# Two score tiles summed in turn at a change of token group, and one weight read issued earlier

## The chip, the cores and the metric

The kernel runs on one core of a Trainium2 chip. The metric is the time of one execution on the device in microseconds (us), the median of several runs. A profile is taken of one execution; its span goes from the first to the last instruction. Engines are called PE (TensorE, matmuls), DVE (VectorE), ACT (ScalarE), POOL (GpSimd, here mostly indirect gathers) and SP (SyncE, here the queue that issues almost all other DMAs).

## The reference

A layer norm, then the sum of the input, an attention with one key/value head and 32 query heads, and a product-key mixture of experts with 32 heads and two experts of 4096 per head and token. S = 2048 tokens, D = 512.

```python
x = A_x
xn = _layernorm(x, axis=-1)
return x + _A_ref(xn, A_wq, A_wk, A_wv, A_wo) + _B_ref(xn, B_w_q, B_k1, B_k2, B_u, B_v)

# _A_ref: softmax(q k^T * Dh**-0.5) v, 32 query heads of 16, one k and one v, then wo
# _B_ref
s1 = jnp.einsum("nhd,ed->nhe", q1, k1)          # 64 keys each
s2 = jnp.einsum("nhd,ed->nhe", q2, k2)
i1 = jnp.argsort(-s1, axis=-1)[..., :K]         # K = 2
i2 = jnp.argsort(-s2, axis=-1)[..., :K]
...
g = _softmax(top_s, axis=-1)
act = _gelu(jnp.einsum("nd,nhkd->nhk", xf, u[top_e]))
out = jnp.einsum("nhk,nhk,nhkd->nd", g, act, v[top_e])
```

## The kernel before, in words

**Tokens, groups, chunks.** The 2048 tokens are 16 tiles of 128, in four groups (`ph` 0 to 3) of four tiles (`GT` = `TPH` = 4). The expert scores of a group are made in eight chunks (`c`) of four heads: the query projection and the keys are folded beforehand into one weight of 512 columns per chunk (`wp_make`), which is kept as a high and a low part, written to DRAM (`d_w`) and read again by `wp_read` for the later groups. A chunk's weight is four tiles `wk`, one per quarter of D (`KC` = 4), out of eight buffers.

**One score tile** (`item`, lines 513 to 550) is one token tile against one chunk: four quarters `k` of three matmuls each (`TERMS`: high x high, high x low, low x high; line 532) into one PSUM tile `psc` of 128x512. It needs `XT[g][k]`, the transposed normed tokens of the group (tile `xt`, four buffers, one per quarter), and `WC[n_][k]`, the chunk's weights. Then DVE takes eight `max` (line 545) and eight `max_index` (line 547), and behind the group's fourth tile `batch` combines the results into expert numbers and gates. `psc` comes out of a PSUM pool of three buffers (tag "x") which the other helpers share.

**The order of the chunks** is `SEQ`: group 0 chunks 0 to 7, group 1 chunks 0 and 1, group 2 chunks 0 to 7, group 1 chunks 2 to 7, group 3 chunks 0 to 7. Groups 0 and 1 (`NSP` = 2) use their experts by gathers of u and v rows (POOL, line 883) with DVE dot products (895) and adds (930). Groups 2 and 3 are computed densely over all experts by `dense`, behind their eighth chunk: one-hot matmuls for the gates, then 32 blocks of `pact` (line 799) and, two blocks behind each other, `pout` in `sums` (line 783).

**The hand-written order.** From line 1147 on, PE, ACT, DVE, POOL and SP run in the order in which the program emits. The loop runs over 256 attention steps. A step emits scores `sc` (318), ACT's exps `pt` (321), `pv` (332), `mid` (DVE's expert work), scores again, and at its end `fill`, which takes work from the generator `score_thread` until a budget (`aim`, at most `MOST` = 4.0 per step) is spent. The generator yields the cost of each piece, 3 x `UNIT` for a quarter. A `yield None` ends the fill of this step whatever is left in the budget.

**A turn.** While the last tile of a group's run of chunks is summed, each quarter `k` that is done frees `xt` `k`, and `load_phase2_xt` (line 994) issues the load of the next group's `xt` on SP behind it. Lines 1012 and 1013 then end the step by a `yield None` (the rest) before the next group's first tile. This holds for three turns: group 0 to 1, 1 to 2, 1 to 3. It does not hold where `dense` comes next.

**Behind the dense blocks of group 2** the chunk `after` (group 1, chunk 2) follows. Its first two weight tiles are read at the last block (line 807), its other two at the very end of `dense` (lines 862 to 864):

```python
        yield from sums()
        if after is not None:
            wp_read(after, range(2, KC))
```

SP issues DMAs strictly in the order of emission, and its queue also carries the attention's small loads and stores: `qa` (305 to 310), sums and outputs of a unit (350, 356), `rc` (365), `dinv` (371), `rsb` (376), `wo` (392).

Of the kernel before, what the change touches and what calls it, by code (L numbers as in the profile page):

```python
# [23 lines left out]
P = 128  # L24
# [4 lines left out]
E = 64  # L29
NT = S // P  # L30
GT = 4
NGRP = NT // GT
KC = D // P
NC = 8
TPH = GT
NPH = NGRP
NSP = 2
# [13 lines left out]
UNIT = 0.235  # L51
# [3 lines left out]
def tile_kernel(ctx, tc, x, wq, wkv, wo, wqT, kT, uv, ub, vb, out):  # L55
    nc = tc.nc
# [7 lines left out]
    start = start_stack.enter_context(tc.tile_pool(name="start", bufs=1))  # L64
# [55 lines left out]
    xtile = lambda name: ps.tile([P, 512], F32, name=name, tag="x", bufs=3)  # L120
# [3 lines left out]
    XT, XN, ACC, XP = {}, {}, {}, [None]  # L124
# [60 lines left out]
    TERMS = ((0, 0), (0, 1), (1, 0))  # L185
# [278 lines left out]
    WC = {}  # L464
# [37 lines left out]
    def wp_read(n, ks=range(KC)):  # L502
        for k in ks:
            wk = wk_tile()
            nc.sync.dma_start(raw(wk[:]), d_w[SEQ[n][1]][:, k])
            WC.setdefault(n, []).append(wk)

    SEQ = ([(0, c) for c in range(NC)] + [(1, c) for c in range(2)] + [(2, c) for c in range(NC)]
           + [(1, c) for c in range(2, NC)] + [(3, c) for c in range(NC)])
    M8, I8 = {}, {}  # L510
    BT = 4

    def item(n_, ti, make=()):
        ph, c = SEQ[n_]
        nph, nc_ = SEQ[n_ + 1] if n_ + 1 < len(SEQ) else (None, None)
        t = TPH * ph + ti
        g, j = divmod(t, GT)
        b, jb = divmod(ti, BT)
        if jb == 0:
            m8 = small.tile([P, BT, 8, 8], F32, name="m8", bufs=1)  # L520
            i8 = small.tile([P, BT, 8, 8], U32, name="i8", bufs=1)
            M8[ph, c, b], I8[ph, c, b] = m8, i8
        m8, i8 = M8[ph, c, b], I8[ph, c, b]
        p = xtile("psc")

        last = ti == TPH - 1
        more = nc_ is not None and not (ph >= NSP and c == NC - 1)
        read = more and n_ + 1 >= NC
        n = 0
        for k in range(KC):  # L530
            for a, bb in TERMS:
                nc.tensor.matmul(p, XT[g][k][:, a, j * P:(j + 1) * P], WC[n_][k][:, bb, :],  # L532
                                 start=n == 0, stop=n == 11)
                n += 1
            if read and ti == 0 and k < 2:
                wp_read(n_ + 1, range(2 * k, 2 * k + 2))
            if last and more and nph != ph:
                load_phase2_xt(nph, k)
            if k < KC - 1:
                yield 3 * UNIT  # L540
            if k == 1:

                yield from islice(make, 1)
        for s in range(8):
            nc.vector.max(m8[:, jb, s, :], p[:, s * E:(s + 1) * E])  # L545
        for s in range(8):
            nc.vector.max_index(i8[:, jb, s, :], m8[:, jb, s, :], p[:, s * E:(s + 1) * E])  # L547
        if jb == BT - 1:
            batch(ph, c, b)
        yield 3 * UNIT  # L550

    IDX, G = {}, {}
# [9 lines left out]
                DT.append(da[:, i, :].rearrange("p (t r s) -> p t r s", t=GT, r=2))  # L562

    def batch(ph, c, b):
        m8, i8 = M8.pop((ph, c, b)), I8.pop((ph, c, b))
        sh = [P, BT, 4]
        T = lambda name, dt=F32, s=sh, bufs=1: small.tile(s, dt, name=name, bufs=bufs)
        mv = m8.rearrange("p t (h s) k -> p t h s k", s=2)
        a1, a2, b1, b2 = mv[:, :, :, 0, 0], mv[:, :, :, 0, 1], mv[:, :, :, 1, 0], mv[:, :, :, 1, 1]
        s1, c1, c2, cond = T("s1"), T("c1"), T("c2"), T("cond")  # L570
        V = nc.vector
        V.tensor_add(s1, a1, b1)
        V.tensor_add(c1, a1, b2)
        V.tensor_add(c2, a2, b1)
        V.tensor_tensor(out=cond, in0=c1, in1=c2, op=OP.is_ge)
        mx = T("mx")
        V.tensor_max(mx, c1, c2)
        V.tensor_sub(mx, mx, s1)
        ex = T("ex")

        def exp_later(gates):

            def go():
                nc.scalar.activation(ex, mx, AF.Exp)
                behind(gates)

            LATER.append(go)

        fi = T("fi", F32, [P, BT, 8, 2])
        V.tensor_copy(fi, i8[:, :, :, 0:2])  # L590
        fv = fi.rearrange("p t (h s) k -> p t h s k", s=2)
        i1a, i1b, i2a, i2b = fv[:, :, :, 0, 0], fv[:, :, :, 0, 1], fv[:, :, :, 1, 0], fv[:, :, :, 1, 1]
        e1, e2 = T("e1"), T("e2")
        stt = V.scalar_tensor_tensor
        den = T("den")
        if ph < NSP:
            idx = T("idx", I32, [P, BT, 4, 2], NIDX)
            stt(idx[:, :, :, 0], i1a, float(E), i2a, op0=OP.mult, op1=OP.add)
            stt(e1, i1a, float(E), i2b, op0=OP.mult, op1=OP.add)
            stt(e2, i1b, float(E), i2a, op0=OP.mult, op1=OP.add)  # L600
            V.tensor_sub(e1, e1, e2)
            V.tensor_mul(e1, e1, cond)
            V.tensor_add(idx[:, :, :, 1], e1, e2)
            gg = T("gg", F32, [P, BT, 4, 2], NIDX)

            def gates():
                V.tensor_scalar(den, ex, 2.0, 2.0, op0=OP.mult, op1=OP.add)
                V.reciprocal(gg[:, :, :, 0], den)
                V.tensor_mul(gg[:, :, :, 1], ex, gg[:, :, :, 0])
                G[ph, c] = gg  # L610

            exp_later(gates)
            for jb in range(BT):
                IDX[ph, c, b * BT + jb] = idx[:, jb].rearrange("p h k -> p (h k)")
            return
        w = slice(8 * c, 8 * c + 8)
        if c == 0:
            DT.clear()
            dense_tiles()
        df1, df2, dgt = DT[:3]  # L620
        ii = T("ii", F32, [P, 2, BT, 8])
        for n, (p0, p1, q0) in enumerate(((i1b, i1a, i1a), (i2a, i2b, i2a))):
            o = ii[:, n].rearrange("p t (h k) -> p t h k", k=2)
            V.tensor_copy(o[:, :, :, 0], q0)
            V.tensor_sub(e1, p1, p0)
            V.tensor_mul(e1, e1, cond)
            V.tensor_add(o[:, :, :, 1], e1, p0)
        hi = T("hi", F32, [P, BT, 8])
        V.tensor_scalar(hi, ii[:, 1], 32.0, None, op0=OP.is_ge)
        for r in range(2):  # L630
            stt(df1[:, :, r, w], hi, 64.0, ii[:, 0], op0=OP.mult, op1=OP.add)
            stt(df2[:, :, r, w], hi, -32.0, ii[:, 1], op0=OP.mult, op1=OP.add)

        def gates():
            V.tensor_scalar(den, ex, 2.0, 2.0, op0=OP.mult, op1=OP.add)
            gg = T("gd", F32, [P, BT, 8])
            gv = gg.rearrange("p t (h k) -> p t h k", k=2)
            V.reciprocal(gv[:, :, :, 0], den)
            V.tensor_mul(gv[:, :, :, 1], ex, gv[:, :, :, 0])
            gh = T("gh", F16, [P, BT, 8])  # L640
            V.tensor_scalar(gh, gg, GS, None, op0=OP.mult)
            V.tensor_copy(dgt[:, :, 0, w], gh)
            stt(dgt[:, :, 1, w], gg, GS, gh, op0=OP.mult, op1=OP.subtract)

        exp_later(gates)


    def dense(DG, after):
# [60 lines left out]
        for n, src in enumerate((df1, df2, dgt)):  # L709
            if n == 2:  # L710
                yield None
            p = xtile("ptd")
# [60 lines left out]
        def sums():  # L773

            used[0] += 2
            if formed[0] < used[0]:
                flush()
            for j in range(GT):
                p = xtile("pout")
                n = 0  # L780
                for wd, vs in ready:
                    for a, c in TERMS:
                        nc.tensor.matmul(p, wd[:, a, j * P:(j + 1) * P], vs[:, c, :], start=n == 0, stop=n == 5)  # L783
                        n += 1
                acc = ACC[GT * DG + j]
                nc.vector.tensor_add(acc, acc, p)  # L786
                yield 6 * UNIT
# [3 lines left out]
        for b in range(NB):  # L791
# [4 lines left out]
            n = 0  # L796
# [58 lines left out]
            if b % 2:  # L855
# [3 lines left out]
                else:  # L859
                    yield None  # L860
                ready, held = held, []
        yield from sums()
        if after is not None:
            wp_read(after, range(2, KC))
        OUTS.extend(range(GT * DG, GT * DG + GT))


# [133 lines left out]
    def score_thread():  # L1001
        for n, (ph, c) in enumerate(SEQ):
            if n < 2:
                yield from wp_make(c)
            make = wp_make(n + 1) if 0 < n < NC - 1 else iter(())
            for ti in range(TPH):
                yield from item(n, ti, make)
                yield from islice(make, 1)
            yield from make
            WC.pop(n)  # L1010
            if n + 1 < len(SEQ) and SEQ[n + 1][0] != ph and not (ph >= NSP and c == NC - 1):
                yield None
            if ph >= NSP and c == NC - 1:
                yield from dense(ph, n + 1 if n + 1 < len(SEQ) else None)
                dense_on[0] = 0
# [246 lines left out]
```

## Time and profile before

| | |
|---|---|
| median of three runs | 1997.14 us (1992.95, 1997.14, 2001.03) |
| the profiled execution | 2001.03 us, its span 1999.3 us, mean granted clock 0.967 |
| DVE busy | 1682.7 us (84% of the span) |
| ACT busy | 1292.0 us (65%) |
| POOL busy | 570.8 us (29%) |
| score matmuls `psc` | 1536, 388.2 us in all |
| `pv` and `sc` matmuls of the attention | 4096 and 2048, 524.1 and 389.1 us |

A timeline row reads: start in us, length in us, engine, line, operation, output<-inputs, shapes, count, and in brackets the idle time of the engine before it with what ended that. A row of SP (SPq) is the issue of DMAs, not their transfer. A windows row reads: stretch, its length, then busy us of PE, PEld (weight loads, which overlap PE), DVE, ACT and POOL with counts, the granted TensorE clock, the DMA engines' busy share, and GB/s. In the chain of work that ended last, PE has 63% of the span and DVE 20%. The row `psc` of the groups' list names 5.3 us of idle time in front of it, 3.2 of them ended by the load of `xt`.

### The profile page before, as it was taken

To read this page: it belongs to the slowest core of one execution; us is meant where nothing else is said; L and a number is where in the kernel's file an instruction comes from. 1 tells how busy PE (TensorE), PEld (TensorE's weight loads), DVE (VectorE), ACT (ScalarE), POOL (GpSimd) and SP (SyncE) were. 2 spreads that over 40 slices of the span, in tenths; PEclk is the share of its full clock that TensorE was granted. 3 is DMA by queue.
4 is the path that set the end of the run, shared out by engine and by line. 5 is a ranking of instruction groups with operands and counts; after the bars stand their busy time and mean duration, and the time that the engine had idled before them with its cause. 6 is when DMAs were issued, how large, how long until landed. Compare 5 with 4: busy or idle time off the path is not lost.

```text
span 1999.3 us, 34729 instructions
## 1 busy us (share of the span) xinstructions
PE 1882.9 (94%) x10990; PEld 997.5 (50%) x10990; DVE 1682.7 (84%) x6713; ACT 1292.0 (65%) x1804; POOL 570.8 (29%) x542
## 2 busy tenths in 40 slices
PE   6869999999998998999999999999899789999997
PEld 4534444555554444555555455555445345555552
DVE  7537888999998786999999779999999668999993
ACT  3236666655556785787877565555568567788873
POOL 2202232222222232333444222222223333333320
PEclk9989999999997998999999999999979899999999
DMA  7847878977664878888889877777568877888762
GB/s 272 301 185 235 276 272 272 331 275 248 218 212 140 229 221 271 264 269 269 284 297 328 286 253 261 268 238 225 176 169 234 276 245 263 268 277 257 263 211 63
DMA packets 239882, 494.79 MB, mean 247 GB/s; under 512 B 93380, under 2 KB 93380, under 8 KB 239692
## 3 DMA queue, kind: packets, MB, share of 16 engines
q0 software_dynamic: 73728, 268.47, 40.5%
q1 hardware_dynamic: 163960, 222.44, 34.0%
q10 hardware_dynamic: 2004, 1.61, 0.3%
q8 instruction: 88, 1.44, 0.3%
q14 instruction: 102, 0.84, 0.1%
HBM read 429.51 MB, written 57.64 MB: 244 GB/s over the span
## 4 chain that ended last, share of the span: by engine, by line
PE 63%; DVE 20%; DMA 5%; issue 2%; ACT 2%; SPq 1%; DVEq 0%; ACTq 0%
PE pv L332 18%; PE sc L318 12%; PE psc L532 10%; PE pout L783 8%; PE pact L799 8%; DVE i L547 5%; DVE xa L930 4%; DVE m L545 3%; DVE g L895 3%; PE pg L752 3%; PE pw L487 2%; PE pwo L427 1%; DMA dg<-gst 1%; ACT pt L321 1%; DMA fin<-dpart 1%
## 5 line engine op out<-in xcount | busy, mean ns | idle before, releaser
L321 ACT ACTIVATE pt<-sc 128x1024 f32<-128x1024 f32 x1024 | 993.0, 1025 | 471.1 <-PE sc L318 424.6
L883 POOL DMA_INDIRECT g<-in_uv_dram,idx x512 | 554.0, 1082 | 1358.4 <-DVE xa L930 697.4
L332 PE MATMUL pv<-pt,vaug 128*32 128x512 f32 x4096 | 524.1, 631 | 0.0
L318 PE MATMUL sc<-qa,kaug 64*128 64x512 f32 x2048 | 389.1, 454 | 14.4 <-ACT pt L321 13.5
L532 PE MATMUL psc<-wk,xt 128*128 128x512 f32 x1536 | 388.2, 400 | 5.3 <-DMA xt<-dxt 3.2
L930 DVE SCALAR_TENSOR_TENSOR xa<-g,w,xa 128x512 f32<-128x512 f32 x512 | 370.6, 745 | 0.0
L895 DVE CUSTOM_DVE_ANT_0 g<-g,xa 128x512 f32<-128x512 f32 x512 | 336.1, 681 | 3.0 <-DMA g<-in_uv_dram,idx 3.0
L532 PEld LDWEIGHTS psc<-wk,xt 128*128 128x128 f32 x1536 | 277.8, 188 | 108.7 <-issue 38.5
L318 PEld LDWEIGHTS sc<-qa,kaug 64*128 64x128 f32 x2048 | 157.6, 187 | 338.2 <-ACT pt L321 203.5
L332 PEld LDWEIGHTS pv<-pt,vaug 128*32 128x32 f32 x4096 | 110.7, 113 | 263.4 <-issue 261.7
L799 PE MATMUL pact<-xt,wk 128*128 128x512 f32 x768 | 198.7, 404 | 14.6 <-DVE fin L433 6.3
L547 DVE FIND_INDEX8 i<-m,psc 128x8 uint32<-128x64 f32 x1024 | 206.4, 221 | 0.0
L783 PE MATMUL pout<-wk,wd 128*128 128x512 f32 x768 | 195.7, 402 | 8.7 <-DVE wd L835 4.7
L799 PEld LDWEIGHTS pact<-xt,wk 128*128 128x128 f32 x768 | 141.1, 190 | 65.4 <-issue 17.7
L783 PEld LDWEIGHTS pout<-wk,wd 128*128 128x128 f32 x768 | 140.6, 188 | 56.7 <-DVE wd L835 6.0
L545 DVE MAX8 m<-psc 128x8 f32<-128x64 f32 x1024 | 146.0, 214 | 22.2 <-PE psc L532 19.8
L786 DVE TENSOR_TENSOR da<-da,pout 128x512 f32<-128x512 f32 x128 | 82.7, 679 | 8.2 <-PE pout L783 7.9
L918 DVE SCALAR_TENSOR_TENSOR w<-gth,ga 128x4 f32<-128x4 f32 x128 | 20.2, 158 | 79.9 <-ACT gth L911 79.4
L688 DVE TENSOR_TENSOR wk<-rw,wk 128x512 fp32r<-128x512 f32 x128 | 84.8, 682 | 0.1
L725 DVE TENSOR_TENSOR oh<-oh 128x2048 f16<-128x2048 f16 x64 | 78.0, 1219 | 7.1 <-PE pg L752 7.1
L752 PE MATMUL pg<-oh 128*128 128x32 f16 x1024 | 73.4, 246 | 8.1 <-DVE oh L728 8.1
L687 ACT CAST wk<-rw 128x512 fp32r<-128x512 f32 x128 | 73.6, 628 | 9.0 <-DMA rw<-in_ub_dram 6.7
(150 smaller groups left out, 1341.8 us busy)
## 6 DMA issues: line engine op xcount, KB each, us to landing
wk<-dw SPq DMA_DIRECT2D x96, 512.0 KB
wqt<-in_wqT_dram SPq DMA_DIRECT2D x32, 512.0 KB
dw<-wk SPq DMA_DIRECT2D x32, 512.0 KB
rw<-in_ub_dram SPq DMA_DIRECT2D x64, 256.0 KB
rw<-in_vb_dram SPq DMA_DIRECT2D x64, 256.0 KB
dg<-gst SPq DMA_DIRECT2D x32, 512.0 KB
gy<-dg SPq DMA_DIRECT2D x64, 256.0 KB
qa<-dqh SPq DMA_DIRECT2D x128, 64.0 KB
```

The lines of the kernel that those rows point to most:

```text
L318: nc.tensor.matmul(p[:, b, :], kaug[o:o + 64, kc * P:(kc + 1) * P], QA[u][o:o + 64, i, :], start=True, stop=True)
L321: nc.scalar.activation(pt, p, AF.Exp, scale=SCALE)
L332: nc.tensor.matmul(PV[u][32 * j:32 * j + 32, :], vaug[:, kc, :], pt[:, b, :], start=kc == 0, stop=kc == 15)
L532: nc.tensor.matmul(p, XT[g][k][:, a, j * P:(j + 1) * P], WC[n_][k][:, bb, :], start=n == 0, stop=n == 11)
L545: nc.vector.max(m8[:, jb, s, :], p[:, s * E:(s + 1) * E])
L547: nc.vector.max_index(i8[:, jb, s, :], m8[:, jb, s, :], p[:, s * E:(s + 1) * E])
L752: nc.tensor.matmul(p[:, i * NB:(i + 1) * NB], oa[:, :, i], ob[:, :, i], start=True, stop=True)
L783: nc.tensor.matmul(p, wd[:, a, j * P:(j + 1) * P], vs[:, c, :], start=n == 0, stop=n == 5)
L799: nc.tensor.matmul(p, us[:, a, k * P:(k + 1) * P], XT[DG][k][:, c, :], start=n == 0, stop=n == 11)
L883: nc.gpsimd.indirect_dma_start(out=gt, out_offset=None, in_=uv, in_offset=bass.IndirectOffsetOnAxis(ap=IDX[ph, c, ti][:, s:s + 1], axis=0))
L895: nc.vector.tensor_tensor_reduce(u, u, XN[TPH * ph + ti], scale=1.0, scalar=0.0, op0=OP.mult, op1=OP.add, accum_out=a[:, i:i + 1])
L930: nc.vector.scalar_tensor_tensor(acc, v, w[:, i:i + 1], acc, op0=OP.mult, op1=OP.add)
```

## The change

`item` takes a tuple of tiles instead of one. At a turn, the last two tiles of the last chunk go through it together: for each quarter `k`, three matmuls for the third tile, three for the fourth, then the load of the next group's `xt` `k`; the two PSUM tiles are held side by side, and the maxima of both follow behind the last quarter. The `yield None` behind a turn is removed. All other tiles go one by one, as before. In `dense`, the read of the second pair of weight tiles stands in front of the last `sums` instead of behind it.

```diff
-    def item(n_, ti, make=()):
+    def item(n_, tis, make=()):
...
-        p = xtile("psc")
-        last = ti == TPH - 1
+        ps_ = [xtile("psc") for _ in tis]
+        last = tis[-1] == TPH - 1
...
         for k in range(KC):
-            for a, bb in TERMS:
-                nc.tensor.matmul(p, XT[g][k][:, a, j * P:(j + 1) * P], WC[n_][k][:, bb, :],
-                                 start=n == 0, stop=n == 11)
-                n += 1
-            if read and ti == 0 and k < 2:
+            for p, ti in zip(ps_, tis):
+                for n, (a, bb) in enumerate(TERMS):
+                    nc.tensor.matmul(p, XT[g][k][:, a, ti * P:(ti + 1) * P], WC[n_][k][:, bb, :],
+                                     start=k == 0 and n == 0, stop=k == KC - 1 and n == len(TERMS) - 1)
+                if ti != tis[-1]:
+                    yield 3 * UNIT
+            if read and tis[0] == 0 and k < 2:
                 wp_read(n_ + 1, range(2 * k, 2 * k + 2))
             if last and more and nph != ph:
                 load_phase2_xt(nph, k)
...
-        for s in range(8):
-            nc.vector.max(m8[:, jb, s, :], p[:, s * E:(s + 1) * E])
-        for s in range(8):
-            nc.vector.max_index(i8[:, jb, s, :], m8[:, jb, s, :], p[:, s * E:(s + 1) * E])
-        if jb == BT - 1:
-            batch(ph, c, b)
+        for p, ti in zip(ps_, tis):
+            for s in range(8):
+                nc.vector.max(m8[:, ti, s, :], p[:, s * E:(s + 1) * E])
+            for s in range(8):
+                nc.vector.max_index(i8[:, ti, s, :], m8[:, ti, s, :], p[:, s * E:(s + 1) * E])
+        if last:
+            batch(ph, c, 0)
...
@@ dense
-        yield from sums()
         if after is not None:
             wp_read(after, range(2, KC))
+        yield from sums()
...
@@ score_thread
-            for ti in range(TPH):
-                yield from item(n, ti, make)
+            turn = n + 1 < len(SEQ) and SEQ[n + 1][0] != ph and not (ph >= NSP and c == NC - 1)
+            for tis in ((0,), (1,), (2, 3)) if turn else ((0,), (1,), (2,), (3,)):
+                yield from item(n, tis, make)
                 yield from islice(make, 1)
             yield from make
             WC.pop(n)
-            if n + 1 < len(SEQ) and SEQ[n + 1][0] != ph and not (ph >= NSP and c == NC - 1):
-                yield None
```

More of the change, by code (lines that the diff above doesn't have):

```diff
@@ L511, in tile_kernel @@
     BT = 4
-    def item(n_, ti, make=()):
+    def item(n_, tis, make=()):
         ph, c = SEQ[n_]
         nph, nc_ = SEQ[n_ + 1] if n_ + 1 < len(SEQ) else (None, None)
[L516 to L519, printed above, removed]
+        g = ph
+        if tis[0] == 0:
             m8 = small.tile([P, BT, 8, 8], F32, name="m8", bufs=1)
             i8 = small.tile([P, BT, 8, 8], U32, name="i8", bufs=1)
-            M8[ph, c, b], I8[ph, c, b] = m8, i8
-        m8, i8 = M8[ph, c, b], I8[ph, c, b]
-        p = xtile("psc")
-        last = ti == TPH - 1
+            M8[ph, c], I8[ph, c] = m8, i8
+        m8, i8 = M8[ph, c], I8[ph, c]
+        ps_ = [xtile("psc") for _ in tis]
+        last = tis[-1] == TPH - 1
         more = nc_ is not None and not (ph >= NSP and c == NC - 1)
         read = more and n_ + 1 >= NC
-        n = 0
         for k in range(KC):
-            for a, bb in TERMS:
-                nc.tensor.matmul(p, XT[g][k][:, a, j * P:(j + 1) * P], WC[n_][k][:, bb, :],
-                                 start=n == 0, stop=n == 11)
-                n += 1
-            if read and ti == 0 and k < 2:
+            for p, ti in zip(ps_, tis):
[5 more added lines that the diff above has]
+            if read and tis[0] == 0 and k < 2:
                 wp_read(n_ + 1, range(2 * k, 2 * k + 2))
@@ L564, in batch @@
     def batch(ph, c, b):
-        m8, i8 = M8.pop((ph, c, b)), I8.pop((ph, c, b))
+        m8, i8 = M8.pop((ph, c)), I8.pop((ph, c))
         sh = [P, BT, 4]
```

## The prediction

> **What bounds the kernel now.** I read the busy totals first, then the PE timeline round the three places that the change touches, then SP's and DVE's rows there, then the windows behind them.
>
> ```profile
> PE 1882.9 (94%) x10990; PEld 997.5 (50%) x10990; DVE 1682.7 (84%) x6713; ACT 1292.0 (65%) x1804; POOL 570.8 (29%) x542
> 450.00:600.00 150.00, 150.00 (x860) 83.08 (x860) 146.70 (x977) 85.94 (x104) 36.60 (x37) 1.00 0.70 226
> 1300.00:1440.00 140.00, 140.00 (x802) 77.71 (x804) 136.79 (x900) 80.35 (x98) 34.32 (x34) 1.00 0.67 220
> ```
>
> PE is the bound: 94% of the span, and in the two long scoring stretches it is never idle (150.00 of 150, 140.00 of 140; columns are stretch, PE, PEld, DVE, ACT, POOL, clock, DMA share, GB/s). DVE is a close second there (146.70 and 136.79). So time can only come from places where PE sits idle. The groups' turns are such places. There are three: from group 0 to 1 (turn 1), from 1 to 2 (turn 2, two chunks later), from 1 to 3 (turn 3).
>
> ```profile
> 379.67 1.92 PE L332 MATMUL pv<-pt,vaug 128*32 128x512 f32 x16
> 381.53 0.73 PE L318 MATMUL sc<-qa,kaug 64*128 64x512 f32 x4
> 383.23 0.49 PE L318 MATMUL sc<-qa,kaug 64*128 64x512 f32 x2 [0.97 <-ACT pt L321]
> 384.14 0.49 PE L318 MATMUL sc<-qa,kaug 64*128 64x512 f32 x2 [0.42 <-ACT pt L321]
> ...
> 424.52 1.66 PE L532 MATMUL psc<-wk,xt 128*128 128x512 f32 x6
> ...
> 429.39 2.35 PE L532 MATMUL psc<-wk,xt 128*128 128x512 f32 x9
> 433.51 2.34 PE L532 MATMUL psc<-wk,xt 128*128 128x512 f32 x9 [1.77 <-DMA xt<-dxt]
> ```
> ```profile
> 1266.82 0.96 PE L532 MATMUL psc<-wk,xt 128*128 128x512 f32 x3
> 1267.84 0.51 PE L318 MATMUL sc<-qa,kaug 64*128 64x512 f32 x2
> 1268.75 0.50 PE L318 MATMUL sc<-qa,kaug 64*128 64x512 f32 x2 [0.41 <-ACT pt L321]
> ...
> 1275.53 2.32 PE L532 MATMUL psc<-wk,xt 128*128 128x512 f32 x9 [1.48 <-DMA xt<-dxt]
> ```
>
> Turn 1's rest leaves an attention step with no score matmuls, and PE waits for ACT: 0.97 + 0.42. Turn 2's rest cuts a step to 6 score matmuls and costs nothing itself; but the fourth quarter of the next group comes 1.77 late. Turn 3 loses 0.41 behind its rest and 1.48 for the same load. In all 1.39 + 1.77 + 1.89 = 5.05 us, 0.25% of the span: all that the first edit can take away directly.
>
> **The change part by part.** *What moves.* In the built programs ACT's and POOL's orders are unchanged. PE's differ in attention steps 33 to 44 (turns 1 and 2) and 158 to 163 (turn 3) of 256 only, DVE's and SP's in the same places, and SP's also at the second edit. The counts are the same: nothing is added, so the price is in waits alone. Steps of 0, 18, 18, 18 score matmuls become 15, 15, 15, 18; a quarter (3 matmuls) takes 3.63/15 x 3 = 0.725 us (a fill of 15 runs from 375.38 to the next row at 379.01).
>
> *When the loads go out and land.*
>
> ```profile
> 377.07 2.39 SPq L998 DMA_DIRECT2D xt<-dxt  x4
> ...
> 425.50 1.02 SPq L998 DMA_DIRECT2D xt<-dxt  x2
> ...
> 1262.38 5.75 SPq L998 DMA_DIRECT2D xt<-dxt  x4
> ```
>
> From the SP queue's packet records (a load ends in sixteen 4-byte packets) I read landings. Alone, 512 KB land 3.0 us after issue (377.07 to 380.04, 420.76 to 423.83). With gathers on the DMA engines too, loads land 2.56 us apart (1267.32, 1269.88, 1272.44, 1275.00), and the fourth of a turn 8.5, 7.2 and 7.2 us after its issue (387.61, 433.37, 1275.00). After the change quarter k of the old xt is free after quarter k of both last tiles, so the first three loads go out 0.7 to 5.5 us sooner. The fourth still leaves only after the very last quarter, and without a rest its user is 3 quarters behind.
>
> *Turn 1:* the last quarter ends with step 32 at 379.0, as before. The new group starts behind attention at 382.2, needs its fourth load at 382.2 + 3 x 0.725 = 384.4. Loads two to four leave at about 376.2, 377.6, 379.1; of the three, about 1.5 are through when gathers start at 380.0 (one of four was, starting 0.9 later), the rest take 1.5 x 2.56: landed 383.8. No wait, 0.6 to spare. Gain 1.39; ACT's exps of that step are hidden under 3.63 us of score matmuls.
>
> *Turn 2:* step 39 starts at 421.34 - 1.39 + 3 x 0.24 = 420.7 (three matmuls more are behind it than before). Its fill, from 423.9, holds the last quarter and four of the new group; the fourth load leaves at 424.6 + 0.15 and is wanted at 426.8. The rsb load, ahead of it on SP, goes out about 1.5 us sooner than at 421.85 and is through; gathers brought data from 429.0. So it lands after 3.0 us, 427.75: a wait of 1.0. Bounds: 0.8 (no issue delay) and 5.1 (7.2 as before). I take 1.0, since the queue is empty then.
>
> *Turn 3:* the last quarter is the first of step 158's fill and ends at 1267.55; the fourth load leaves by 1267.75 and is wanted at 1269.7. Gathers are in flight, so I take the shared rate: start of data 0.95 after issue, 2.56 for the transfer, some 0.2 behind: 1271.5, a wait of 1.8. Bounds: 1.0 (3.0 alone) and 5.2 (7.2). This one eats turn 3's 1.89.
>
> *PE in sum:* -5.05 + 0 + 1.0 + 1.8 = -2.25 us.
>
> *DVE.* Two tiles are now reduced behind each other, after the second. One tile's max and index take 2.66 us (tile to tile, 377.86 to 380.52). In turn 1 DVE was ready at 377.86 and now waits for 378.4: 0.55 lost. DVE sat idle for PE and ACT at 396.26 (0.70), 420.08 (1.37), 424.00 (0.58), 434.51 (0.73): 3.4, of which the three PE waits, 2.8, go as scores come sooner. 2.8 - 0.55 = 2.25 covers PE's gain of turns 1 and 2 with nothing over. PSUM: two of three score buffers are held for 8 quarters; the next group's first tile takes the third, its second tile starts a step later (6.8 us in turns 1 and 2; 0.7 + the wait in turn 3), when DVE, which in turn 3 is free of the earlier tile's 2.66 us, has just let go. Cost 0, bounds 0 to 2.66 once, in turn 3.
>
> *Second edit.* It acts once, behind group 2's dense blocks. Two 512 KB loads leave SP at about 1094 instead of 1104 to 1106, in front of rsb and wo. They were in time before: PE went from the last output sums to the scores at 1110.38 with no wait. Gain 0. Behind them on SP the rsb load (1100.49) waits for dinv's landing anyway; if their 1 MB delays it by 2 x 1.5 us, its user on DVE (L381 at 1111.18) still has some 5 us. Cost 0; bounds -0.3 and +2.
>
> *Sum.* The profiled execution took 2001.03 (span 1999.3 and 1.7 round it), 3.9 over the median of 1997.14. -2.25 makes it 1998.8, and the median 1994.9.
>
> *A clock price.* Waits can cost more than themselves:
>
> ```profile
> 601.41 0.68 PE L318 MATMUL sc<-qa,kaug 64*128 64x512 f32 x2 [0.94 <-ACT pt L321]
> 602.33 0.55 PE L318 MATMUL sc<-qa,kaug 64*128 64x512 f32 x2 [0.24 <-ACT pt L321]
> 602.80 3.51 PE L332 MATMUL pv<-pt,vaug 128*32 128x512 f32 x16
> ```
>
> Behind 1.2 us of waiting the 16 pv matmuls take 3.51 instead of 1.92 (granted clock 0.58 from 602 to 606). The 1.39 at 383 had no such follower, nor 1.48 at 1275 (1.00 in both). So each new wait costs 0 to 1.6 more; I take 0, by the nearest rows in size and place. The Trainium skill (TensorE: Matmul & The Clock Gate, "What's actually happening") says that the clock halves only after at least one idle window of about 3.4 us. By that rule neither new wait could cost it and the sum stays; the row at 602.80 contradicts it. With 1.6 for each of the two new waits the sum would be +0.95.
>
> **The rivals.**
> - *The fourth load stays as late as it was (slower).* If it again lands 7.2 us after issue in turns 2 and 3, the waits are 5.1 + 5.2 = 10.3, less 5.05: +5.3; both exceed 3.4 us and would halve the clock once each, 1.6 each: +8.5. 2002.4 to 2005.6. It decides from a mean landing of 4.7 us after issue. For it: 8.5, 7.2 and 7.2 measured. Against: in those, two or three loads issued within 2.4 us stood ahead of it; now they left 1.5 us apart, the first a step earlier.
> - *DVE becomes the bound (no change).* It ran 146.70 of 150, and before the dense blocks PE waits for its last batch:
>
> ```profile
> 1451.04 1.97 PE L714 MATMUL ptd<-ident,da 128*128 128x128 f32 x8 [8.69 <-DVE da L631]
> ```
>   If DVE ends its scores no sooner, PE's gain becomes a longer wait there and at 607.69 (0.72 now): 1997.1. For it: a balance of 2.25 gained by DVE against 2.16 gained by PE in turns 1 and 2. Against: PE's own idle of 0.00 behind each turn.
> - *All of it (faster).* The fourth loads arrive in time: -5.05, 1992.1. Against: 3.0 us is the fastest landing seen, 2.2 are there.
> - *Nothing of it shows:* that is the second edit, within every case above.
>
> **How the numbers follow.** The sum 0.42; late load 0.18; DVE 0.18; all of it 0.17; something unseen 0.05. The three runs before lie 8 us apart, so a median of three may be off by some 3. Predicted 1994.9. 80%: down from 1992.1 to 1988, up to 2005, which leaves half of the clock's price and the unseen out. 0.5% (10 us) is about what a measurement of this kernel tells from no change: faster would be below 1987.2, slower above 2007.1. No case lies there by its own price. Faster gets a quarter of "all of it" (rests that halve the clock in executions other than the profiled one) and most of the unseen, 0.08; slower a third of the late load (the clock halved for longer than one stretch) and the rest, 0.08; the same 0.84.
>
> **What would show it.** The ACT waits behind sc in steps 33 and 158 gone; one wait for xt in front of the fourth quarter in turn 2 (about 1.0) and in turn 3 (about 1.8), none in turn 1; the waits at the first ptd of both dense parts unchanged within 0.5; no wait for wk in front of group 1's third chunk, as now. A xt wait over 4 us, half clock behind a turn, or ptd waits grown by 2 would make the sum wrong.

## The result and the profile after

The changed kernel is slower. Its median is 2008.61 us over 20 runs (1998.77 to 2020.54), that of the kernel before 1997.45 over as many (1992.61 to 2009.10): a ratio of 1.005, 95% interval 1.0032 to 1.0068, or about +10 us (the two medians lie 11.2 apart). The prediction was 1994.9, range 1988 to 2005.

Line numbers of the changed kernel stand one lower or one higher than before (532 is 531, 918 is 919), those of the experiments up to ten higher. The page of the changed kernel: the chain of work that ended last, and the group of score matmuls (busy us, mean ns, idle time in front of them and what ended most of it).

```profile
PE 56%; DVE 25%; DMA 6%; issue 3%; ACT 2%; SPq 1%; ACTq 0%; DVEq 0%
...
L531 PE MATMUL psc<-wk,xt 128*128 128x512 f32 x1536 | 393.7, 403 | 11.6 <-DMA xt<-dxt 7.1
```

PE's share of the chain falls from 63 to 56%, DVE's rises from 20 to 25; the idle time in front of the score matmuls is 11.6 us instead of 5.3, of which the load of `xt` ended 7.1 instead of 3.2. PE's timeline at the three turns, in order:

```profile
387.31 2.50 PE L531 MATMUL psc<-wk,xt 128*128 128x512 f32 x9
391.51 2.35 PE L531 MATMUL psc<-wk,xt 128*128 128x512 f32 x6 [1.70 <-DMA xt<-dxt]
393.79 1.22 PE L318 MATMUL sc<-qa,kaug 64*128 64x512 f32 x4
394.94 2.24 PE L332 MATMUL pv<-pt,vaug 128*32 128x512 f32 x16
...
436.89 0.96 PE L531 MATMUL psc<-wk,xt 128*128 128x512 f32 x3 [1.38 <-DMA xt<-dxt]
...
1280.73 0.93 PE L531 MATMUL psc<-wk,xt 128*128 128x512 f32 x3 [0.69 <-DMA xt<-dxt]
1285.05 2.93 PE L531 MATMUL psc<-wk,xt 128*128 128x512 f32 x6 [3.38 <-DMA xt<-dxt]
1287.91 1.22 PE L318 MATMUL sc<-qa,kaug 64*128 64x512 f32 x4
```

The ACT waits behind `sc` are gone, but PE now waits 1.70 + 1.38 + 0.69 + 3.38 = 7.15 us for `xt`. Behind two of these waits, 1.70 and 3.38, the granted clock halves (called half clock below): four `sc` matmuls take 1.22 instead of 0.73. DVE at the same places (turn 2, then turn 3):

```profile
431.98 0.16 DVE L919 SCALAR_TENSOR_TENSOR w<-gth,ga 128x4 f32<-128x4 f32 x1 [4.33 <-ACT gth L912]
...
1278.71 1.15 DVE L546 MAX8 m<-psc 128x8 f32<-128x64 f32 x8 [1.28 <-PE psc L531]
...
1286.73 1.15 DVE L546 MAX8 m<-psc 128x8 f32<-128x64 f32 x8 [3.36 <-PE psc L531]
```

DVE waits 4.33 us for ACT's tanh in turn 2 and 1.28 + 3.36 us for score tiles in turn 3.

Most of the program isn't touched, and there one execution differs from the next by 10 us and more (1560.6 us outside the stretches below in the changed kernel, 1537.4 in the run e1 of the next section, which has the same program there). So I compare the stretches that hold the turns: attention steps 31 to 64 (turns 1 and 2) and 154 to 184 (turn 3), cut where a step's first exp begins on ACT. The last lines of the windows views over these stretches (sum of the lengths, then busy us of each engine in them), first of before, then of after:

```profile
sum 448.60, PE 434.81 PEld 240.66 DVE 430.71 ACT 253.46 POOL 109.10; mean PE 86.96 PEld 48.13 DVE 86.14 ACT 50.69 POOL 21.82
```
```profile
sum 458.20, PE 439.59 PEld 241.43 DVE 430.62 ACT 254.06 POOL 109.22; mean PE 87.92 PEld 48.29 DVE 86.12 ACT 50.81 POOL 21.84
```

They grew by 9.6 us, about the measured loss of 10. On PE's side the account closes: 4.8 us are busy time (439.59 - 434.81 for the same 2487 matmuls), 4.8 idle (18.6 instead of 13.8). Of the busy part, 4.1 lie in steps 31 to 64 and 154 to 165, where the clock was halved for 10.2 us and before not at all. The other 0.6 lies in steps 165 to 184, where after has no more half clock than before (7.2 us, 8.1 before); it isn't explained. The idle part is +3.90 of `xt` waits (7.15 - 3.25), -1.80 of ACT waits, and +2.77 of waits for DVE: 1.11 in front of `psc` at 562.84, 0.44 + 0.96 at 1364.18 and 1413.79, and 0.26 more at the first `ptd` behind turn 3 (8.95 after 8.69). DVE did the same work to within 0.1 us and sat idle 9.7 longer.

### The profile page after: what moved, and what is told of

Read it like the earlier page. It is cut to its first block, busy times and chain, and to the rows that moved or that the text cites. A ratio compares the mean times of both kernels' runs of the same rounds, so it can differ in the third digit from the quotient of the medians.

```text
span 2018.8 us, 34729 instructions
## 1 busy us (share of the span) xinstructions
PE 1887.7 (94%) x10990; PEld 1003.3 (50%) x10990; DVE 1682.7 (83%) x6713; ACT 1292.1 (64%) x1804; POOL 573.6 (28%) x542
## 4 chain that ended last, share of the span: by engine, by line
PE 56%; DVE 25%; DMA 6%; issue 3%; ACT 2%; SPq 1%; ACTq 0%; DVEq 0%
PE pv L332 15%; PE sc L318 11%; PE psc L531 9%; PE pout L784 8%; PE pact L800 7%; DVE i L548 5%; DVE xa L931 5%; DVE g L896 4%; DVE m L546 3%; DMA dg<-gst 2%; DVE oh L726 2%; PE pg L753 2%; PE pw L487 2%; PE pwo L427 1%; ACT pt L321 1%
## 5 line engine op out<-in xcount | busy, mean ns | idle before, releaser
L332 PE MATMUL pv<-pt,vaug 128*32 128x512 f32 x4096 | 512.9, 619 | 0.0
L531 PE MATMUL psc<-wk,xt 128*128 128x512 f32 x1536 | 393.7, 403 | 11.6 <-DMA xt<-dxt 7.1
L548 DVE MATCH_VALUE_LOAD i<-m,psc 128x8 f32 x1024 | 81.4, 79 | 0.0
```

What stands on the lines that cost most here:

```text
L332: nc.tensor.matmul(PV[u][32 * j:32 * j + 32, :], vaug[:, kc, :], pt[:, b, :], start=kc == 0, stop=kc == 15)
L531: nc.tensor.matmul(p, XT[g][k][:, a, ti * P:(ti + 1) * P], WC[n_][k][:, bb, :], start=k == 0 and n == 0, stop=k == KC - 1 and n == len(TER ...
L548: nc.vector.max_index(i8[:, ti, s, :], m8[:, ti, s, :], p[:, s * E:(s + 1) * E])
```

## The experiments

In this table "xt waits" is PE's waiting for the token loads in the three turns, "half" the time at half clock in the steps 31 to 64 and 154 to 165, the two lengths are those of the stretches above, from one profile each, and the ratio is to the kernel before, run beside it. The third line runs before's own program in the turns and differs from before by 0.5 and 0.2 us there: that much is noise. All times in us.

| kernel | xt waits | half | steps 31–64 | steps 154–184 | ratio, 95% interval |
|---|---|---|---|---|---|
| before | 3.25 | 0 | 231.8 | 216.8 | |
| after | 7.15 | 10.2 | 234.9 | 223.3 | 1.005 [1.0032, 1.0068] |
| e1 second edit only | 3.38 | 0 | 232.3 | 217.0 | 0.9983 [0.9962, 1.0003] |
| e2 rest put back | 0 | 0 | 232.3 | 215.5 | 0.9974 [0.9949, 0.9998] |
| e3 rest taken away only | 11.10 | 13.6 | 240.2 | 222.3 | 1.0071 [1.0047, 1.0096] |
| e4 fourth load left out | 1.05 | 0 | 231.8 | 217.5 | 0.9979 [0.9949, 1.0009] |
| e6 maxima in one bunch | 2.88 | 0 | 233.3 | 216.8 | 0.9990 [0.9964, 1.0016] |
| e5 gathers held | 7.85 | 6.8 | 235.8 | 222.2 | 1.0030 [1.0009, 1.0051] |
| e8 gathers held sooner | 7.29 | 10.2 | 234.8 | 222.9 | 1.0037 [1.0012, 1.0063] |
| e10 before, gathers held | 1.24 | 3.4 | 231.4 | 216.9 | 0.9984 [0.9957, 1.0011] |
| e11 no burst of gathers | 2.49 | 0 | 231.4 | 218.0 | 0.9984 [0.9965, 1.0003] |
| e7 buffers lent, all turns | 1.08 | 0 | 228.6 | 217.6 | 1.0032 [1.0004, 1.0059] |
| e9 buffers lent, turns 1, 2 | 1.28 | 0 | 228.5 | 216.7 | 1.0005 [0.9983, 1.0026] |
| e12 lent for a shorter time | 0 | 0 | 229.3 | 215.7 | 0.9977 [0.9955, 0.9999] |

**The parts of the change.** e1 is before with the second edit alone; e2 is after with the rest back; e3 is before without its rest, tiles one by one.

```diff
# e1, on before
-        yield from sums()
         if after is not None:
             wp_read(after, range(2, KC))
+        yield from sums()
# e2, on after
             WC.pop(n)
+            if turn:
+                yield None
# e3, on before
-            if n + 1 < len(SEQ) and SEQ[n + 1][0] != ph and not (ph >= NSP and c == NC - 1):
-                yield None
```

> The second edit alone: the two weight loads in front of the last sums, the turns as before. If the loss sits in the turns (late fourth load, or DVE starved by the bunched tiles), this run equals the kernel before: ratio 1.000 within 0.003, no wait of the scores for wk behind group 2's dense blocks, as before. If the second edit costs (its 1 MB in front of rsb and wo on SP), it is slower by some 5 us (ratio 1.0025), with a wait of DVE's L381 for rsb or of PE's L427 for wo that before does not have.

> The changed kernel with the rest put back behind each turn: two tiles in turn, then the step ends. Theory late load: the rest gives the fourth load an attention part (3.2 us) more, the waits for xt (1.70, 1.38, 0.69 + 3.38 in the changed kernel) fall under 1 in sum, and the time comes to that of before or 2 us under it (ratio 0.998 to 1.000). Theory bunching: DVE gets no finished tile for 8 quarters and then two at once, so its idle time round the turns stays some 5 us above that of before, and so does the time (ratio 1.0025) although no load is waited for.

> The kernel before without the rest: the last tiles one by one, the next group straight behind. Theory late load: all four loads go out within the last tile's four quarters and are wanted 3 quarters later, so the waits for xt are longer than in the changed kernel, 4 us or more per turn, DVE idles with PE, and the run is slower than the changed kernel (ratio to before 1.006 or more). Theory bunching: DVE gets its tiles evenly, the run is as fast as before or faster (0.997 to 1.000).

The second edit costs nothing that shows. With the rest, the in-turn order does what it was written for: no wait for `xt` is left in any turn. Without the rest PE waits in all three, in either order. So the removed rest carries the loss, and the in-turn order softens it (11.10 to 7.15 us of waits). e2 also shows the limit of the gain: PE's 1.77 of turn 2 are gone, yet steps 31 to 64 are no shorter.

**What the time follows.** e4 leaves out the fourth load of each turn, so that the next group's fourth quarter of scores is made of the old group's tokens. e6 is before, with the third tile's maxima at a turn kept back and taken together with the fourth's: the bunching alone, no other part of the change.

```diff
# e4, on after
             if last and more and nph != ph:
-                load_phase2_xt(nph, k)
+                if k < KC - 1:
+                    load_phase2_xt(nph, k)
+                else:
+                    XT[nph].append(XT[g][k])
# e6, on before (maxima() holds the two loops of max and max_index)
+        if ti == TPH - 2 and more and nph != ph:
+            KEPT.append(maxima)
+        else:
+            while KEPT:
+                KEPT.pop(0)()
+            maxima()
```

> The changed kernel, but at a turn the fourth quarter of xt is not loaded again: the next group reads the old group's fourth quarter (that quarter of its scores is computed from other tokens, and three loads of 512 KB are left out). Theory late load: no wait for the fourth quarter, at most 0.7 for the third, no half clock behind it; the sum of the prediction without its two waits, 3 to 5 us under before (ratio 0.998). Theory bunching: DVE's idle time round the turns stays some 4 us above that of before, ratio 1.002 or more, with PE waiting for no load.

> The kernel before with one thing of the change alone: the maxima of the third tile of a turn's last chunk are held until the fourth tile is summed; the tiles are still summed one by one, and the rest stays. Theory bunching: DVE runs out of work for want of a finished tile, waits for ACT's tanh behind an attention step, and idles 2 to 4 us more in steps 31 to 64 than the 9.3 us of before, with steps 31 to 64 as much longer than 231.8. Rival (bunching is free): DVE's idle time and the steps stay within 1 us of before, ratio 1.000.

In e4 PE waits for nothing in turns 1 and 2, 3.1 us less than before, and the stretch is as long as before (231.8). PE's gain comes back as waits for DVE (2.0 us in front of `psc` at 506.9 and 557.3), and DVE's timeline says why (before, then e4):

```profile
424.00 0.16 DVE L918 SCALAR_TENSOR_TENSOR w<-gth,ga 128x4 f32<-128x4 f32 x1 [0.58 <-ACT gth L911]
...
426.24 0.16 DVE L922 SCALAR_TENSOR_TENSOR w<-gth,ga 128x4 f32<-128x4 f32 x1 [4.33 <-ACT gth L915]
```

The wait of 4.33 stands in the changed kernel too, at 431.98. With the third tile finished only along with the fourth, DVE has no maxima to take in that step, comes 4.33 us too early to the product that needs ACT's tanh, and ACT's place for the tanh is behind the step's exps. Before, this wait was 0.58. e6 has the bunching and nothing else: the wait is 4.68 there, and steps 31 to 64 are 1.4 longer. DVE's idle time in them rises by 1.6, less than the 2 to 4 expected (9.27 to 10.89). So the in-turn order pays with DVE's time what it gives to PE.

**What makes the loads late.** SP's and POOL's rows of the changed kernel (issue, not transfer):

```profile
376.75 7.81 SPq L999 DMA_DIRECT2D xt<-dxt  x4
...
433.48 0.31 SPq L999 DMA_DIRECT2D xt<-dxt  x1
...
1267.83 11.19 SPq L999 DMA_DIRECT2D xt<-dxt  x4
```
```profile
1272.10 1.20 POOL L884 DMA_INDIRECT g<-in_uv_dram,idx  x1 [9.26 <-DVE xa L931]
1273.61 0.97 POOL L884 DMA_INDIRECT g<-in_uv_dram,idx  x1 [0.30 <-issue]
1274.88 0.94 POOL L884 DMA_INDIRECT g<-in_uv_dram,idx  x1 [0.30 <-DVE ga L907]
1276.12 0.94 POOL L884 DMA_INDIRECT g<-in_uv_dram,idx  x1 [0.30 <-issue]
```

The fourth loads leave at 384.24, 433.48 and 1278.70; by the packet records they land at 391.04, 436.50 and 1284.51, that is 6.8, 3.0 and 5.8 us later. In turns 1 and 3 a burst of gathers moves data meanwhile; in turn 2 none does (the gathers' queue is empty from 430 to 438). Three runs hold the gathers back round a turn (e5 and e8 in the changed kernel, e10 in before):

```diff
# e5, on after; e8 sets it a tile sooner, at tis[0] == 1 of the three chunks; e10 the same on before
+        if len(tis) > 1:
+            hold[0] = 1
...
+            if tis[0] == 0 and k == 2:
+                hold[0] = 0
...
-                    gathers(4)
+                    if not hold[0]:
+                        gathers(4)
```

> The changed kernel, but no gather is issued from the turn's first quarter until the next group's first tile has its third quarter; they follow later, at most four a step. Theory that the shared DMA engines make the fourth load late: it lands some 3 us after issue, the waits for xt fall from 7.2 us in sum (1.70, 1.38, 4.07) to 2 to 3, and steps 31 to 64 and 154 to 184 take 4 to 5 us less than the 234.9 and 223.3 us of the changed kernel together; ratio to before about 1.001 to 1.002. Rival (the loads are late by their own issue and landing time, whoever shares): the waits stay within 1 us of 7.2 and the ratio at 1.005.

> The changed kernel, gathers held back again, but from the second tile of the turn's last chunk on, four quarters sooner than in e5, where a burst of four gathers was still issued under the loads (1259.25 to 1263.27 in front of turn 3's last two). Theory that a burst of gathers makes the fourth load late: with none in flight each load lands about 3.0 us after issue; the waits for xt fall from 7.2 us in sum to at most 3 (about 0 to 1 per turn), no half clock behind a turn, and steps 31 to 64 and 154 to 184 take 452 us or less, against 458.2 in the changed kernel and 448.6 before; ratio about 1.001. Rival (late by themselves): waits of 6 us or more again, ratio 1.003 or more.

> The kernel before, rest and all, with the gathers held back from the third tile of a turn's last chunk until the next group's first tile has its third quarter. Theory that gathers make the fourth load late: the waits for xt of before (1.77 and 1.48) go, steps 31 to 64 and 154 to 184 take 1 to 3 us less than 448.6 together; ratio 0.999, which the times alone can't tell from 1. Rival: waits as before, or DVE waits for a gather that is now late, which shows as a wait of DVE for g.

They missed. A gather is emitted long before it runs (it waits for the adds that free its buffer), so the burst of turn 3 had been emitted before the hold, and ran under the loads as it had done (1259.25 to 1263.27 in e5, 1259.98 to 1263.99 in e8). They say nothing for or against the gathers. e11 takes the transfers away instead and leaves POOL's order, the buffers and every wait as they are; the terms of fourteen of the 512 expert slots become zero.

```diff
# e11, on after; QUIET: slots 70 to 74, 83 to 86 and 319 to 323
         gt = gtile()
-        nc.gpsimd.indirect_dma_start(
+        if m in QUIET:
+            nc.gpsimd.memset(gt, 0.0)
+        else:
+            nc.gpsimd.indirect_dma_start(
```

> The changed kernel, but fourteen of the 512 expert gathers (the five that run round each of turns 1 and 3 and the four round turn 2) are replaced by a memset of their tile on POOL, so those experts' terms are zero; order, buffers and all waits stay. Theory A (gathers in flight make the loads of xt late): all xt loads land about 3.0 us after issue, so PE's waits for xt fall from 7.15 us to under 3 (about 0.9 per turn), no half clock behind turns 1 and 3, steps 31 to 64 near 232 (234.9 with the gathers) and 154 to 184 near 218 (223.3). Rival B (the lateness is the empty lead of three quarters and the loads' own rate, not the gathers): waits stay at 6 to 7 us and the two stretches at 234 to 235 and 222 to 223. Theory C beside A (DVE is the bound): even if the waits are gone, steps 31 to 64 do not come below before's 231.8 by more than 1.

PE's timeline of e11: the two `xt` waits that are left (turns 2 and 3), the wait for DVE between the turns, and the first `ptd` behind turn 3. Then DVE's row of turn 2, and the windows' sum over the same steps.

```profile
426.90 0.96 PE L532 MATMUL psc<-wk,xt 128*128 128x512 f32 x3 [1.27 <-DMA xt<-dxt]
...
552.91 0.96 PE L532 MATMUL psc<-wk,xt 128*128 128x512 f32 x3 [1.18 <-DVE i L549]
...
1265.75 1.67 PE L532 MATMUL psc<-wk,xt 128*128 128x512 f32 x6 [1.22 <-DMA xt<-dxt]
...
1446.91 1.33 PE L716 MATMUL ptd<-ident,da 128*128 128x128 f32 x5 [8.95 <-DVE da L633]
```
```profile
422.11 0.16 DVE L923 SCALAR_TENSOR_TENSOR w<-gth,ga 128x4 f32<-128x4 f32 x1 [4.34 <-ACT gth L916]
```
```profile
sum 449.40, PE 435.39 PEld 240.07 DVE 429.88 ACT 254.01 POOL 109.12; mean PE 87.08 PEld 48.01 DVE 85.98 ACT 50.80 POOL 21.82
```

This splits the loss in two. The gathers in flight make the loads late: without their transfers the waits are 0, 1.27 and 1.22, no clock halves behind a turn, and the stretches are 8.8 us shorter than after (458.2 to 449.4). What is left is the change as the prediction saw it, with about the waits that it forecast for PE (2.49 for 2.8), and it is worth nothing: 449.4 against 448.6 before, ratio 0.9984. DVE's 4.34 and the waits on DVE are still there: PE waits 2.6 us less for `xt` and ACT than before, and 2.8 more for DVE. The run lightens the DMA load of these steps as a whole, so it doesn't say by which part of their way the gathers hold the loads up. Theory C of the expectation holds as well as theory A; rival B fell.

**Versions that might beat both.** If a load is to have more lead, it needs a buffer sooner. e7 lends two gather buffers to `xt` and issues the loads one tile earlier, with tiles one by one and no rest; e9 does so for turns 1 and 2 only, with turn 3 as in before; e12 gives the buffers back sooner and takes turn 3 from e2.

```diff
# e7, on e3
-            if last and more and nph != ph:
-                load_phase2_xt(nph, k)
+            if ti >= 2 and k < 2 and more and nph != ph:
+                load_phase2_xt(nph, 2 * (ti - 2) + k, (ti == 2) == (nph != 2))
+            if ti == 2 and k == 0 and n_ in (6, 22):
+                held[0] = 2
+            if ti == 0 and k == 0 and n_ == 18:
+                held[0] = 0
...
-        while g_next[0] < NSL and g_next[0] < a_next[0] + NGB - lent[0] and most > 0:
+        while g_next[0] < NSL and g_next[0] < a_next[0] + NGB - lent[0] - held[0] and most > 0:
...
-    def load_phase2_xt(g, k):
+    def load_phase2_xt(g, k, borrowed=False):
...
+        if borrowed:
+            xt = gtile(F32R, (P, 2, 512), "xt")
# e12, on e2's turn 3: quarters of the old group's last tile in turn 2, and the end of the loan
+        ks = (2, 3, 0, 1) if last and n_ == 9 else (0, 1, 2, 3)
-        for k in range(KC):
+        for k in ks:
...
+            if n_ == 7 and tis[0] >= 2 and k < 2:
+                load_phase2_xt(nph, 2 * (tis[0] - 2) + k, tis[0] == 2)
+            if n_ == 9 and (tis[0] == 2 and k < 2 or tis[0] == 3 and k >= 2):
+                load_phase2_xt(nph, k)
+            if n_ == 10 and tis[0] == 0 and k == 0:
+                held[0] = 0
```

> No rest, tiles one by one, and two more buffers for the next group's xt, borrowed from the gathers' twelve from the chunk before the turn until group 2 has gone (and from turn 3 to the end), so that the loads go out from the third tile on. Theory late load plus bunching, with DVE as the bound: no wait for xt in any turn, DVE gets its tiles evenly, its idle time in steps 31 to 64 falls from 9.3 to about 6 and in 154 to 184 from 8.6 to about 6; the time is 4 to 6 us under before (ratio 0.997 to 0.998). Rival (PE's idle time in the turns is worth nothing in any form): ratio 1.000. If ten gather buffers are too few, DVE waits for g and it is slower.

> As e7 (no rest, one by one, loads into two borrowed gather buffers), but for turns 1 and 2 only; turn 3 is that of the kernel before, rest included, so that all twelve gather buffers are back for the last third. If e7's gain in steps 31 to 64 (228.6 us against 231.8) is real and its loss came from ten buffers behind turn 3 (steps 193 to the end 466 us against 459), this run takes 228 to 229 and 216 to 218 in the two stretches and is 2 to 4 us faster than before (ratio 0.998 to 0.999), the loss behind step 193 gone. Rival (the loss of e7 was something else): ratio 1.002 or more again.

> Candidate: in turn 1 the next group's first two quarters of xt are loaded a tile early into two gather buffers; in turn 2 the next group's first two quarters go a tile early into the two xt buffers that this frees, and the last tile of the old group is summed in the order 2, 3, 0, 1, so that the other two buffers come free half a tile sooner; the gather buffers go back at the end of chunk 9. Turn 3 as in the run with rest and in-turn sums; second edit as changed. Theory (turns 1 and 2 lose what their xt waits and the in-turn order cost DVE; ten gather buffers up to group 2's end were what cost the earlier borrowing run its gain): steps 31 to 64 228.5 (231.8 before), steps 130 to 154 168.0 as before (175.6 in the earlier run), steps 154 to 184 215.5 (216.8 before), together 4.6 us or 0.23% faster: ratio 0.9977. Rival (the 6.4 us wait for the dxn load behind the dense blocks came from something else, or gathers short of buffers early cost later): 130 to 154 stays near 175 and the ratio is 1.000 or above.

Turns 1 and 2 gain 3.2 to 3.3 us in e7 and e9: no `xt` wait, no rest, and no bunching, so DVE's idle time falls too (from 9.28 to 6.64 in e7). No run here got more out of the first idea in these steps. But both lose it elsewhere: steps 130 to 154 take 175.7 and 175.6 us instead of 168.0, where gathers with ten buffers run behind, and the token load that is issued along with them comes late behind the dense blocks. DVE of e9:

```profile
1093.42 0.69 DVE L902 CUSTOM_DVE_ANT_0 g<-g,xa 128x512 f32<-128x512 f32 x1 [6.37 <-DMA xa<-dxn]
```

e12, whose loan ends with turn 2, keeps the gain of the turns (229.3 and 215.7, 3.7 us less than before together) and takes 170.7 in steps 130 to 154, just above the 166.5 to 170.0 of the versions without lent buffers. Its ratio of 0.9977 is the one expected, but that is luck in part: in its profile the three stretches are together 1.0 us shorter than before (615.6 for 616.6) and not the 4.6 forecast. e2 has 0.9974. Neither is shown to be faster: e1 and e10, whose stretches are as long as before's to within 0.7 us, come out at 0.9983 and 0.9984, and the runs don't tell these four apart.

One more pattern runs through all fourteen profiles: steps 165 to 184 take 138.0 to 138.1 us in each kernel that rests in turn 3 and 139.7 to 140.3 in each that doesn't. The windows of before and after there (length, then busy us of PE, PEld and DVE):

```profile
1315.80:1453.80 138.00, 129.31 (x742) 71.41 (x740) 134.76 (x884) 77.23 (x94) 30.90 (x31) 0.97 0.61 205
1330.90:1471.20 140.30, 129.95 (x742) 71.34 (x740) 137.06 (x904) 77.23 (x94) 32.79 (x33) 0.97 0.60 202
```

DVE is idle for 3.24 us of this stretch in both, and to within 0.01 in all fourteen: its length is DVE's work plus this constant. Without the rest some 2 us of DVE's work come behind step 165 that came ahead of it before (134.8 us busy in the kernels with the rest, 136.4 to 137.1 in those without). So DVE sets the pace there. Why its work comes later without the rest no run here shows.

## Why the prediction was wrong, step by step

- *"PE is the bound", so PE's idle time is time to be had.* This step failed. That PE was never idle in the long stretches was right, but DVE, at 146.70 of 150, had as little room. e4 and e11 removed 3.1 and 1.9 us of PE's waits at turns 1 and 2, and steps 31 to 64 stayed within 0.4 of before; in steps 165 to 184 the length is DVE's busy time and 3.24 in every profile. The rival "DVE becomes the bound", put at 0.18, is what is left of the change once the loads are in time.
- *DVE's balance, 2.25 gained against 2.16 needed.* Only waits that would vanish were counted. The order moves the third tile's maxima behind the fourth tile, and I asked only when the score tiles would be ready, not what DVE would reach instead: the 0.58 wait for the tanh becomes 4.33.
- *Turn 1, no wait.* The fourth load left when forecast (384.24; forecast 379.1 plus the 5.1 by which this execution runs later). But when the gathers started, one of the three loads was through and not one and a half, the other two took 2.9 and 2.7 each, and the matmuls began 0.5 behind the landing: 1.70 instead of 0.6 to spare.
- *Turn 2, a wait of 1.0.* Right: landing 3.0 after issue as forecast, no gathers in the way. The wait was 1.38, since the matmuls began 0.4 behind the landing.
- *Turn 3, a wait of 1.8.* The issue was right (1278.70, less 10.9 for the later start 1267.8; forecast 1267.75), the transfer about right (2.3 for 2.56); "start of data 0.95 after issue" was 3.5. The load waited out the burst of gathers before its first packet moved. With the third load's 0.69 the wait is 4.07.
- *Clock price 0.* Failed: two stretches of half clock, 10.2 us long, cost 4.1 us of PE's time, over two fifths of the loss. The prediction had the row at 602.80 that showed a price and took the two rows that didn't. One of these, the 1.39 us of ACT waits in turn 1, had no price by luck: in e10 the same two waits (0.97 and 0.41) were followed by half clock, and 16 `pv` matmuls took 3.56 instead of 1.92.
- *The ACT waits go.* Right, -1.80.
- *Second edit 0.* Right, within noise (e1).

In terms of the sum: -2.25 forecast; +4.35 on the `xt` waits (7.15 for 2.8), +4.1 of clock, +0.6 of other busy time, +2.8 of waits on DVE make +9.6, and the stretches show +9.6. The rival "late load" named the mechanism, but for turns 2 and 3. There the mean landing was 4.4 us after issue (3.0 and 5.8), short of its deciding point of 4.7; the latest, 6.8, came in turn 1, which it left out. Its price of +5.3 to +8.5 came near by errors that offset each other: the waits were 7.15 and not 10.3, the clock took 4.1 and not up to 3.2, and the 2.8 for DVE weren't in it. I had ranked it low because the loads leave further apart; the loads' own queue wasn't what held them up, the gathers were (e11).

## What to carry to other kernels

When two engines are both near full, an idle gap of one is worth only what the other can follow: price a reorder on both, and for the second ask which wait it will reach early when its work is moved away. A transfer's landing must be forecast with everything that is in flight when it is issued; the fastest landing seen is a floor, not an estimate. What a wait costs at the clock depends on where it falls, so that price belongs into the range even where the nearest rows show none. A pause that looks like waste can be the lead of a load, so before taking it away, find the lead elsewhere (here a lent buffer).

## What the runs showed of the hardware

- A load that SP issues while a burst of gathers drains doesn't share with it at once. In the changed kernel the load issued at 1278.70 moved its first packet at 1282.2, 3.5 us later; between 1279.9 and 1282.0 the gathers' queue moved 202 packets of 4 KB and SP's queue 2, the end of the load before. With no gathers (e11) the first packet came 0.95 after issue (issued at 1262.50, first packet at 1263.45). The Trainium skill (DMA: Bandwidth & Descriptors, "Queues, rings and completion order") says that each DMA engine goes round robin between the queues that have work for it, packet by packet. Once both streams run the trace agrees roughly (311 and 396 packets from 383.0 to 391.1); for the start of the load it doesn't, and no run here shows what holds it.
- The length of a wait alone doesn't decide whether the clock halves. 1.70 us did it in the changed kernel, 1.77 in before and 1.87 in e1 did not. The Trainium skill (TensorE: Matmul & The Clock Gate, "What's actually happening") asks for at least one idle window of about 3.4 us; the 1.70 contradicts that. The clock records of the traces show what the three differ in. In each of the fourteen profiles all changes of the clock lie on one grid of 3.413 us (to within 3 ns; in the changed kernel at 392.2, 395.6, 1283.1 and 1289.9, for example). The 1.70 us lay whole in one piece of that grid; the 1.77 and the 1.87 were cut by a border, with 1.54 and 1.32 in the larger part. In steps 31 to 64 and 154 to 165 of all profiles, each full-clock piece with 1.70 us or more of PE idle (2.76 at most) was followed by half clock, and of those with less only one was: the 1.38 of e10. The same 1.39 in before lay in one piece too, without effect, so the border between the two isn't settled.
